# Splitting the attention burst around a matrix product in a fused attention and feed-forward kernel

## The chip, the cores and the metric

The kernel runs on one core of one Trainium2 chip. The metric is the device time of one execution in microseconds (us), the median over several executions; lower is better. One further execution was taken by the hardware profiler, and all rows shown come from it.

The names of the engines are those of the profile: PE is the matrix engine (its weight loads are listed apart, as PEld), DVE, ACT and POOL are the vector, scalar and general engines, SP is the queue from which most DMAs are issued. Each engine works through its own instructions strictly in the order of the program. They wait for each other by semaphores.

## The reference: what is computed

Sparse attention for 8 batches and 8 heads (576 positions, 64 values a head), followed by a feed-forward layer with a maximum over three products:

```python
scores = scale * np.matmul(q, k.transpose(0, 1, 3, 2))
mask_local = (rel >= 0) & (rel < stride)            # heads 0 to 3, stride 32
mask_strided = (rel >= 0) & (pos[None, :] % stride == pos[:, None] % stride)   # heads 4 to 7
attn = np.exp(scores - max) / (sum + 1e-09)
x = (attn @ v) laid out as 4608 tokens x 512
h = np.maximum(np.maximum(x @ w1, x @ w2), x @ w3)   # 768 wide
out = h @ w_out
```

## The kernel before

**Units.** Attention is cut into 32 units, numbered 0 to 31: a unit is two heads of one batch. In every batch the two strided pairs of heads come first, then the two local ones. One unit goes through these steps:

- `scores(n)` on PE: 32 or 36 small products into the PSUM tile `s_ps` (lines 340 and 318), each of them two passes, so the profile counts 64 or 72.
- `less_maximum(n)` on DVE (lines 361 to 368), `exponentials(n)` on ACT (line 384), `probabilities(n)` and `transposed(n)` on DVE (lines 394 to 404). The last one writes the probabilities to the SBUF tile `pt`. There is one `s_ps` from chunk two on, so the scores of a unit have to wait until the unit before has been transposed.
- `values(n)` on PE: probabilities times values into the PSUM tile `o_ps` (lines 441 and 470, 84 or 64 passes). There is one `o_ps` for all units.
- `leading(n)` on ACT: copies out of `o_ps` into the tokens' places (line 495). `rest(n)` does nothing for units from chunk two on.
- `paired_queries(n)`: for strided units, four ACT copies that lay out the queries (line 295); `scores(n)` reads them.
- `load_qk` and `load_v`: DMAs from SP for a unit two later, each of which waits until the unit whose buffer it takes has been used.

**The feed-forward part** runs in chunks of tokens. Chunks one and two (512 tokens each) are plain: 18 steps `ff_in` of 12 matrix instructions (line 522), each followed by `ff_max` that empties its PSUM bank, and 4 steps `ff_out` (line 552). Everything after that is done in four supers of 896 tokens. A super is 63 products of 6 matrix instructions of 448 columns (line 775, the weights of each come from HBM through `load_next`, eight ahead), then 7 output steps (line 865). Each product's result is copied out by ACT (`snap`, line 818), combined on POOL (line 830) and DVE (line 832). Two PSUM banks, `f_ps`, take turns for all of this.

**How the two are woven.** The order of the program is written out by hand. During chunk two and the supers, one unit of attention at a time is placed between products as a burst. In chunk two the table `first_bursts` gives the step i before which a unit's burst stands (units 8 to 15, two or three steps apart); a super has a burst before its products 8, 18, 28, 38, 48 and 58 (units 16 to 31 in three supers; `COUNTS` gives their number). The function `burst(n)` issues `values(n)`, `scores(n + 1)`, the loads, `leading(n)` and `less_maximum(n + 1)` in that order, and the softmax of unit n + 1 follows behind the next products.

During chunk two, ACT and POOL also build sums of weights for the supers: `build_sums` and `build_mix` on POOL (lines 585 and 593) at the steps of `sums_at`, three steps later `build_high` on ACT (line 603) and `build_low` on POOL (line 609).

## Time and profile before

| what | us |
|---|---|
| median of 3 runs | 690.41 |
| lowest and highest of them | 688.15, 691.15 |
| the profiled execution, whole | 694.4 |
| its span, first to last instruction | 692.7 |
| PE busy in it (94% of the span) | 653.0 |
| DVE, ACT, POOL busy | 376.7, 335.8, 299.6 |

The page of the profile gives, for each engine, the busy time; a chain of work followed back from the last instruction; and groups of instructions with the idle time before them. In a row of the timeline of an engine stand the start, the duration, the engine, the line of the kernel, the operation, its tiles and shape, how many equal instructions follow each other, and in brackets the idle time of the engine before the first of them with what ended it. "issue" there means that nothing in the profile explains the wait. In a row of the view of windows stand the stretch, its length, and for each engine its busy time and, in brackets, the number of its instructions; then the clock that PE was granted (1.00 is full) and two numbers on DMA.

### The profile page before, as it was taken

What the parts mean: (1) busy time and instruction counts of PE and PEld (TensorE: products, weight loads), DVE (VectorE), ACT (ScalarE), POOL (GpSimd) and SP (SyncE); (2) the same over time, 40 slices, a digit from 0 to 9 for tenths busy, and PEclk for the clock granted to TensorE, in tenths of its full rate; (3) what the DMA queues carried; (4) which work ended last, traced back from release to release, by engine and by line L of the source; (5) the groups of instructions that cost most, each with busy time, mean ns of one, the idle gap of its engine ahead of it and who ended that gap; (6) DMA issues with size and microseconds to landing.
All of it is one profiled execution on the core that took longest, in us unless ns stands there. A gap on an engine that the chain in (4) does not pass through costs nothing.

```text
span 692.7 us, 18051 instructions
## 1 busy us (share of the span) xinstructions
PE 653.0 (94%) x7408; PEld 560.6 (81%) x7408; DVE 376.7 (54%) x515; ACT 335.8 (48%) x702; POOL 299.6 (43%) x291
## 2 busy tenths in 40 slices
PE   3679999898999998999999999999999999999997
PEld 3458878686877888888898988889899988999986
DVE  5776965466766664567616556671653264124240
ACT  4757556333444544545555445464444454444441
POOL 8769898569970432322033432201433410444410
PEclk9679999899999999999999999999999999999999
DMA  9799883555778777764168777524867722777411
GB/s 289 201 281 348 283 265 117 173 164 171 241 239 261 248 265 220 248 222 164 62 198 279 241 243 232 171 76 142 251 203 199 214 91 91 214 216 219 142 46 62
DMA packets 89370, 138.36 MB, mean 200 GB/s; under 512 B 10152, under 2 KB 39592, under 8 KB 89288
## 3 DMA queue, kind: packets, MB, share of 16 engines
q1 hardware_dynamic: 85256, 129.86, 60.6%
q10 hardware_dynamic: 4032, 7.34, 2.8%
q8 instruction: 59, 0.97, 0.6%
q14 instruction: 23, 0.19, 0.1%
HBM read 111.21 MB, written 25.95 MB: 198 GB/s over the span
## 4 chain that ended last, share of the span: by engine, by line
PE 76%; DVE 7%; DMA 6%; issue 6%; SPq 2%; ACT 2%; POOL 1%; DVEq 0%; ACTq 0%; POOLq 0%
PE f_ps L775 40%; PE f_ps L865 15%; PE f_ps L522 10%; DMA w<-in_w 5%; PE f_ps L552 4%; PE o_ps L470 2%; PE o_ps L441 2%; PE s_ps L318 2%; PE s_ps L340 1%; DVE h_all L832 1%; POOL snap L830 1%; DVE xc L686 1%; DVE s_ps L397 1%; DVE pt L404 1%; SPq L280 1%
## 5 line engine op out<-in xcount | busy, mean ns | idle before, releaser
L775 PE MATMUL f_ps<-xc,w_stream 128*128 128x448 f32 x1512 | 316.5, 369 | 4.0 <-ACT snap L818 2.3
L775 PEld LDWEIGHTS f_ps<-xc,w_stream 128*128 128x128 f32 x1512 | 283.2, 189 | 31.6 <-ACT snap L818 4.7
L818 ACT COPY snap<-f_ps 128x448 f32<-128x448 f32 x240 | 127.7, 533 | 163.4 <-PE f_ps L775 161.6
L830 POOL TENSOR_TENSOR snap<-snap 128x448 f32<-128x448 f32 x72 | 89.6, 1252 | 161.1 <-ACT snap L818 102.9
L832 DVE TENSOR_TENSOR h_all<-h_all,snap 128x448 f32<-128x448 f32 x96 | 83.0, 907 | 115.9 <-POOL snap L830 115.8
L865 PE MATMUL f_ps<-wNone,h_parts 128*128 128x512 f32 x504 | 115.7, 390 | 0.9 <-ACT h_parts L855 0.9
L830 POOL TENSOR_TENSOR h_all<-snap 128x448 f32<-128x448 f32 x36 | 41.3, 1149 | 164.1 <-ACT snap L818 162.6
L865 PEld LDWEIGHTS f_ps<-wNone,h_parts 128*128 128x128 f32 x504 | 94.3, 188 | 21.5 <-ACT h_parts L855 1.7
L522 PE MATMUL f_ps<-xh,w 128*128 128x512 f32 x288 | 98.7, 416 | 3.4 <-ACT h_max L537 1.9
L522 PEld LDWEIGHTS f_ps<-xh,w 128*128 128x128 f32 x288 | 57.4, 199 | 17.6 <-ACT h_max L537 2.4
L522 PE MATMUL f_ps<-xl,w 128*128 128x512 f32 x144 | 59.0, 410 | 0.4 <-DVE xl L500 0.4
L856 DVE TENSOR_TENSOR h_parts<-h_all,h_parts 128x768 fp32r<-128x768 f32 (+2 forms) x40 | 27.2, 711 | 26.0 <-ACT h_parts L855 25.8
L686 DVE TENSOR_TENSOR xc<-x_block,xc 128x896 fp32r<-128x896 f32 x28 | 29.8, 1086 | 15.5 <-ACT xc L683 15.5
L871 ACT COPY work<-f_ps 128x512 f32<-128x512 f32 x28 | 16.4, 586 | 41.8 <-PE f_ps L865 41.8
L361 DVE TENSOR_TENSOR s_ps<-s_ps,mloc 128x640 f32<-128x640 f32 x14 | 11.6, 831 | 45.4 <-PE s_ps L340 45.3
L522 PEld LDWEIGHTS f_ps<-xl,w 128*128 128x128 f32 x144 | 28.9, 201 | 6.5 <-DVE xl L500 0.7
L404 DVE STREAM_TRANSPOSE pt<-s_ps 128x640 f32<-128x640 f32 (+2 forms) x32 | 32.5, 1016 | 1.1
L855 ACT CAST h_parts<-h_all 128x768 fp32r<-128x768 f32 (+2 forms) x40 | 24.5, 642 | 17.6 <-DVE h_all L832 11.0
L361 DVE TENSOR_TENSOR s_ps<-s_ps,mpair 128x576 f32<-128x576 f32 x14 | 10.7, 765 | 40.3 <-PE s_ps L318 40.3
L384 ACT ACTIVATE s_ps<-s_ps 128x640 f32<-128x640 f32 (+2 forms) x30 | 19.5, 652 | 26.7 <-DVE s_ps L368 26.7
L340 PE MATMUL s_ps<-qk_t 64*32 64x64 f32 (+1 forms) x1408 | 19.8, 227 | 12.7 <-DMA qk_t<-in_kT 8.5
L552 PE MATMUL f_ps<-wNone,hh 128*128 128x512 f32 x96 | 30.7, 400 | 0.0
(87 smaller groups left out, 709.5 us busy)
## 6 DMA issues: line engine op xcount, KB each, us to landing
w_stream<-scratch SPq DMA_DIRECT2D x252, 256.0 KB, 3.8
w<-in_w SPq DMA_DIRECT2D x18, 512.0 KB, 5.4
qk_t<-in_qT SPq DMA_DIRECT2D x28, 288.0 KB, 3.5
qk_t<-in_kT SPq DMA_DIRECT2D x28, 288.0 KB, 3.8
v_t<-in_v_str SPq DMA_DIRECT2D x56, 128.0 KB, 3.5
out<-work ACTq DMA_DIRECT2D x28, 256.0 KB, 2.0
scratch<-w SPq DMA_DIRECT2D x27, 256.0 KB, 3.6
v_t<-in_v_loc SPq DMA_DIRECT2D x48, 96.0 KB, 2.6
```

The source lines that it names most:

```text
L340: pin(nc.tensor.matmul(s_ps[32 * j : 32 * (j + 1), h, k1 : k1 + w], t[hs, q0 : q0 + 32], t[hs, k0 : k0 + w], start=not first, stop=not fir ...
L404: pin(nc.vector.transpose(pt[:, :, : nm * at], s_ps[:, :, : nm * at]))
L522: pin(nc.tensor.matmul(f_ps, w[:, kc, :], x[:, kc, :], start=(kc == 2 and n == 0), stop=(kc == 1 and n == 2)))
L552: pin(nc.tensor.matmul(f_ps, h[:, ts], w, start=(j == 0 and n == 0), stop=(j == NJ - 1 and n == 2)))
L686: pin(nc.vector.tensor_tensor(out=x[m][:, 1], in0=src, in1=x[m][:, 0].bitcast(F32), op=ALU.subtract))
L775: pin(nc.tensor.matmul(out_, w[:, wl, fs], x[:, xl, k, :], start=start and k == 0 and n == 0, stop=k == 1 and n == 2, skip_group_check=not ...
L818: pin(nc.scalar.copy(out=t, in_=src))
L830: pin(nc.gpsimd.tensor_tensor(out=h if i == 0 else u, in0=u, in1=t, op=ALU.add))
L832: pin(nc.vector.tensor_tensor(out=h, in0=h, in1=u, op=ALU.max))
L855: pin(nc.scalar.copy(out=to[:, 0, j0:j1], in_=src))
L856: pin(nc.vector.tensor_tensor(out=to[:, 1, j0:j1], in0=src, in1=to[:, 0, j0:j1].bitcast(F32), op=ALU.subtract))
L865: pin(nc.tensor.matmul(outs[t], h, w, start=(j == 0 and n == 0), stop=(j == NJ - 1 and n == 2)))
```

## The change

`burst` is taken apart. `ahead(n)` now issues the scores of unit n, its load of queries and keys and `less_maximum(n)`; `placed(n)` issues the values of unit n, the load of later values, and `leading(n)`. `ahead(n + 1)` stands where the burst of unit n stood. `placed(n)` stands one step (chunk two) or one product (supers) later. In chunk two, `paired_queries` is also moved ahead of `ff_max`. The work itself is the same, instruction for instruction, apart from two waiting instructions fewer on PE. Unit 15's values keep their place.

```diff
     def ahead(n):
-        if n < len(units):
-            scores(n)
-            list(load_qk(n + 2))
-
-    def burst(n, alone=False):
+
+        scores(n)
+        list(load_qk(n + 2))
+        less_maximum(n)
+
+    def placed(n):
 
         values(n)
-        coming = n + 1 if n + 1 < len(units) and not alone else None
-        if coming:
-            scores(coming)
         list(load_v(n + 2))
         leading(n)
         rest(n)
-        if coming:
-            list(load_qk(coming + 2))
-            less_maximum(coming)
-        return coming
...
     for i in range(3 * NJ + CH // P):
+        if i - 1 in first_bursts and first_bursts[i - 1] < 15:
+            placed(first_bursts[i - 1])
         if i in first_bursts:
-            coming, since = burst(first_bursts[i], first_bursts[i] == 15), i
+            if first_bursts[i] < 15:
+                coming, since = first_bursts[i] + 1, i
+                ahead(coming)
+            else:
+                placed(15)
         if i < 3 * NJ:
             ff_in(1, i // 3, i % 3)
         else:
...
         if coming and i == since + 1:
             probabilities(coming)
             transposed(coming)
+            if (coming + 1) % 4 in (0, 1):
+                paired_queries(coming + 1)
+            coming = None
         if i < 3 * NJ:
             ff_max(1, i // 3, i % 3)
         else:
             ff_store(1, i - 3 * NJ)
-        if coming and i == since + 1:
-            if (coming + 1) % 4 in (0, 1):
-                paired_queries(coming + 1)
-            coming = None
...
         def before(s, k):
 
+            n = 16 + sum(COUNTS[:s]) + k // 10
             if s == 0 and k == 1:
-                scores(16)
-                list(load_qk(18))
-                less_maximum(16)
+                ahead(16)
                 running[:] = [16, k]
             elif k % 10 == 8 and k // 10 < COUNTS[s]:
-                running[:] = [burst(16 + sum(COUNTS[:s]) + k // 10), k]
+                running[:] = []
+                if n + 1 < len(units):
+                    ahead(n + 1)
+                    running[:] = [n + 1, k]
+            elif k % 10 == 9 and k // 10 < COUNTS[s]:
+                placed(n)
 
         def after(s, k):
 
-            if running and running[0]:
+            if running:
                 n, since = running
```

How the rows move, at two places. The first is PE in the first super, around products 27 to 29, where the burst of unit 18 stood (L441 are its values, L340 the scores of unit 19, L775 or L774 the products). Before:

```order
L775 MATMUL f_ps_790<-xc_2972,w_stream 128x448 x6
L441 MATMUL o_ps<-pt,v_t 64x64 x14
L441 MATMUL o_ps<-pt,v_t 64x32 x8
L441 MATMUL o_ps<-pt,v_t 64x64 x14
L441 MATMUL o_ps<-pt,v_t 64x32 x6
L340 MATMUL s_ps<-qk_t 32x64 x36
L775 MATMUL f_ps_791<-xc_2966,w_stream 128x448 x6
L775 MATMUL f_ps_790<-xc_2967,w_stream 128x448 x6
```

The change, at the same place:

```order
L774 MATMUL f_ps_790<-xc_2972,w_stream 128x448 x6
L340 MATMUL s_ps<-qk_t 32x64 x36
L774 MATMUL f_ps_791<-xc_2966,w_stream 128x448 x6
L441 MATMUL o_ps<-pt,v_t 64x64 x14
L441 MATMUL o_ps<-pt,v_t 64x32 x8
L441 MATMUL o_ps<-pt,v_t 64x64 x14
L441 MATMUL o_ps<-pt,v_t 64x32 x6
L774 MATMUL f_ps_790<-xc_2967,w_stream 128x448 x6
```

The scores now stand alone ahead of a product, and the values alone behind it: one stretch of 78 small products (156 passes) has become one of 36 and one of 42.

The second place is ACT near the end of chunk two, steps 14 to 18 (L542 and L537 empty PSUM for `ff_max`, L603 is `build_high`, L384 the exponentials of units 14 and 15, L495 the copies `leading` of units 13 and 14). Before:

```order
L542 CAST hh<-h_max 128x512
L603 CAST sums_high<-work 128x512 x2
L495 COPY x_block_1927<-o_ps 128x192
L495 COPY x_block_2554<-o_ps 128x384
L384 ACTIVATE s_ps<-s_ps 128x2x320
L537 COPY h_max<-f_ps_790 128x512
L495 COPY x_block_1927<-o_ps 128x160
L495 COPY x_block_1927<-o_ps 128x32
L495 COPY x_block_2554<-o_ps 128x128
L495 COPY x_block_2554<-o_ps 128x160
L495 COPY x_block_2554<-o_ps 128x96
L384 ACTIVATE s_ps<-s_ps 128x2x320
```

The next two rows there are again L542 and L603.

The change, from the same row on:

```order
L542 CAST hh<-h_max 128x512
L603 CAST sums_high<-work 128x512 x2
L384 ACTIVATE s_ps<-s_ps 128x2x320
L537 COPY h_max<-f_ps_790 128x512
L495 COPY x_block_1988<-o_ps 128x192
L495 COPY x_block_2616<-o_ps 128x384
L384 ACTIVATE s_ps<-s_ps 128x2x320
L542 CAST hh<-h_max 128x512
L603 CAST sums_high<-work 128x512 x2
L495 COPY x_block_1988<-o_ps 128x160
L495 COPY x_block_1988<-o_ps 128x32
```

The copies of unit 14 (the last rows) now stand behind the second `build_high`, and the exponentials of unit 14 directly behind the first.

## The prediction

> **What bounds the kernel now.** I read the page first: who is busy, what the chain of work that ended last consists of, and the DMA queues.

> ```profile
> PE 653.0 (94%) x7408; PEld 560.6 (81%) x7408; DVE 376.7 (54%) x515; ACT 335.8 (48%) x702; POOL 299.6 (43%) x291
> ...
> q8 instruction: 59, 0.97, 0.6%
> ...
> PE 76%; DVE 7%; DMA 6%; issue 6%; SPq 2%; ACT 2%; POOL 1%; DVEq 0%; ACTq 0%; POOLq 0%
> ```

> PE sets the end; a gain must come out of PE's gaps or its instructions. So next the timeline of PE alone, from chunk two on, for the gaps. These eight stand in or right behind a burst:

> ```profile
> 131.78 0.87 PE L318 MATMUL s_ps<-qk_t,pt 64*64 64x36 f32 x25 [1.87 <-issue]
> 157.11 0.32 PE L340 MATMUL s_ps<-qk_t 64*32 64x64 f32 x8 [1.32 <-issue]
> 247.85 0.54 PE L340 MATMUL s_ps<-qk_t 64*32 64x64 f32 x34 [0.37 <-issue]
> 264.49 2.02 PE L775 MATMUL f_ps<-xc,w_stream 128*128 128x448 f32 x5 [1.76 <-issue]
> 371.72 0.71 PE L318 MATMUL s_ps<-qk_t,pt 64*64 64x36 f32 x34 [0.52 <-issue]
> 401.95 0.68 PE L340 MATMUL s_ps<-qk_t 64*32 64x64 f32 x44 [0.87 <-issue]
> 418.35 0.32 PE L340 MATMUL s_ps<-qk_t 64*32 64x64 f32 x9 [1.27 <-issue]
> 497.47 0.88 PE L775 MATMUL f_ps<-xc,w_stream 128*128 128x448 f32 x3 [0.72 <-ACT snap L818]
> ```

> They come to 8.70 us. Most break off in the middle of equal scores, where no semaphore is waited for. What they are is told by counting PE's instructions from gap to gap in the view of windows (PE and PEld, in brackets):

> ```profile
> 131.78:157.11 25.33, 24.00 (x381) 19.48 (x381) 13.24 (x20) 8.11 (x17) 19.48 (x19) 0.88 0.53 162
> 247.85:264.49 16.64, 14.88 (x251) 13.60 (x252) 10.06 (x14) 6.82 (x16) 5.73 (x5) 0.99 0.70 227
> 371.72:401.95 30.23, 29.36 (x374) 26.15 (x374) 16.13 (x24) 14.27 (x30) 10.01 (x8) 1.00 0.75 244
> 401.95:418.35 16.40, 15.13 (x252) 13.44 (x252) 9.47 (x12) 6.81 (x16) 7.07 (x6) 1.00 0.74 226
> 418.35:497.47 79.12, 77.81 (x751) 67.42 (x750) 46.83 (x60) 40.29 (x78) 15.92 (x14) 1.00 0.56 175
> ```

> The sums are 762, 503, 748, 504 and 1501: 6 to 35 short of 768, 512, 768, 512 and 1536, all multiples of 256, and the rest are PE's waiting instructions, which this view leaves out. The queue of instructions on the page fits: 59 packets for 2 x 7408 instructions are 251 each. So PE's program arrives in blocks of 256, and these gaps are waits for the next block (the last row's label, ACT, names a copy out of the other bank; its place fits the count). A burst of 42 + 36 small products is 312 instructions and takes about 2 us (1.07 and 0.93 for the two halves in rows further down); a product of 12 instructions takes 1.22. Only in a burst are 256 instructions used up faster than they come.

> Two of the gaps cost more than their length. The view of windows has the granted clock, the chain the stretches behind them and undisturbed ones of the same size:

> ```profile
> 131.15:137.97 6.82, 6.18 (x38) 4.95 (x38) 2.29 (x3) 1.68 (x3) 5.67 (x7) 0.50 0.52 137
> 264.27:267.68 3.41, 3.19 (x9) 2.84 (x9) 1.13 (x2) 0.54 (x1) 0.00 (x0) 0.50 0.72 179
> ...
> 132.66 10.90 PE f_ps L522 x36
> 167.81 8.39 PE f_ps L522 x36
> 264.49 13.90 PE f_ps L775 x60
> 280.52 12.48 PE f_ps L775 x60
> ```

> Half the clock behind the gaps of 1.87 and 1.76 us, none behind 1.32: 2.51 + 1.42 us, and the 25 scores in 0.87 us instead of 0.42: 4.4 us together.

> [...] If those dips had another cause, the sum below would lack their 4.4 us.

> **The change part by part.** Three waits in chunk two are for softmax, not for code:

> ```profile
> 164.27 1.17 PE L441 MATMUL o_ps<-pt,v_t 32*64 32x64 f32 x84 [1.14 <-issue]
> 166.40 1.41 PE L318 MATMUL s_ps<-qk_t,pt 64*64 64x36 f32 x64 [0.95 <-ACT pt L295]
> 195.13 1.13 PE L441 MATMUL o_ps<-pt,v_t 32*64 32x64 f32 x84 [0.90 <-issue]
> ...
> 163.32 0.85 DVE L404 STREAM_TRANSPOSE pt<-s_ps 128x640 f32<-128x640 f32 x1
> 164.78 0.62 ACT L542 CAST hh<-h_max 128x512 fp32r<-128x512 f32 x1 [3.95 <-DVE h_max L539]
> ```

> *Code waits.* The scores' and the values' instructions (128 to 168 each) now have a product between them. Two waiting instructions fewer leave the block borders where they were to within two, so those that cut into the scores now cut into the values, with a product ahead of them. The stretch before the border grows by 1.22 us and the 0.19 derived below, 1.41 (two matrix steps, more still, in chunk two). That swallows all gaps but the 1.76, which leaves 0.35; behind the one at 497.47 there was a product ahead of the border already, and I leave 0.30 of it. Gain 8.70 - 0.65 = 8.05. Ends: nothing (the next block is asked for as much later) and 8.70. I take a value near the upper end, because the border moves by a counted number of instructions.

> *Clock.* The longest gap left is 0.35, far under 1.32, behind which the clock held: gain 4.4, ends 0 and 4.4.

> *Waits for softmax.* The values at 164.27 started when the transpose had ended (164.17). Now that the scores stand ahead of the values, a unit's softmax begins 1.07 us earlier against PE, and its successor's scores, which need the same transpose, come where they stood: 1.14 falls to about 0. The queries at 166.40 waited behind `hh`, which waited 3.95 us for DVE; they are moved in front of it: 0.95 to 0. Gain 2.1, ends 0 and 2.1. The third, 0.90, would go likewise, but POOL takes its place:

> ```profile
> 154.81:199.70 44.89, 40.57 (x785) 33.26 (x777) 29.99 (x42) 16.97 (x43) 43.32 (x44) 1.00 0.65 200
> ...
> 184.56 3.18 POOL L593 TENSOR_TENSOR work<-work 128x256 f32<-128x256 f32 x4
> ...
> 187.88 1.14 ACT L603 CAST sums_high<-work 128x512 fp32r<-128x512 f32 x2
> 191.25 0.69 ACT L384 ACTIVATE s_ps<-s_ps 128x640 f32<-128x640 f32 x1 [1.64 <-DVE s_ps L368]
> ...
> 191.97 0.83 DVE L394 TENSOR_REDUCE s_ps<-s_ps 128x10 f32<-128x640 f32 x1 [0.81 <-ACT s_ps L384]
> 194.17 0.85 DVE L404 STREAM_TRANSPOSE pt<-s_ps 128x640 f32<-128x640 f32 x1
> ```

> POOL is busy 43.32 of 44.89 us there, and ACT's `build_high` started 0.14 us after its input was done (187.74). PE will be about 7.0 us earlier by then (1.87 + 0.45 + 2.51 + 1.32 + 2.1, less 1.2 for five splits), while POOL's chain, which follows PE's first steps of chunk two, moves by 1.87 + 0.45 + 2.51 less a split, 4.5. So `build_high` waits until about 183.2. Queued behind it on ACT are the exponentials of unit 14; then DVE must sum, scale and transpose, and PE's scores of unit 15 wait for that: 183.2 + 1.14 + 0.69 + 3.05 (191.97 to 195.02) = 188.1, where PE arrives at 194.23 - 7.0 + 0.19 = 187.4. A wait of 0.7 for one of 0.90: I take no gain, ends -2 and 0.9. Further on, the copies of unit 14 stand behind the next `build_high`, and the values of unit 15 need `o_ps` back; by the same count they are free when PE comes.

> *What splitting costs.* Values stand alone in one place of the trace, the last unit's. The view of windows, cut at products:

> ```profile
> 520.42:521.64 1.22, 1.22 (x7) 1.13 (x6) 1.22 (x3) 0.53 (x1) 0.00 (x0) 1.00 0.76 193
> 521.64:522.95 1.31, 1.31 (x7) 0.94 (x6) 0.27 (x1) 0.53 (x1) 0.00 (x0) 1.00 0.73 224
> 522.95:524.02 1.07, 1.07 (x85) 1.03 (x84) 0.00 (x0) 0.53 (x1) 0.00 (x0) 1.00 0.79 249
> 524.02:525.36 1.34, 1.34 (x12) 1.24 (x7) 0.00 (x0) 0.83 (x4) 0.00 (x0) 1.00 0.75 217
> 525.36:526.60 1.24, 1.24 (x8) 1.13 (x6) 0.00 (x0) 0.53 (x1) 0.38 (x1) 1.00 0.20 23
> ...
> 293.00 1.07 PE o_ps L470 x64
> 294.07 0.93 PE s_ps L318 x64
> ```

> The product ahead of small ones takes 0.09 more, the one behind 0.10. A burst pays that once, its two halves twice: 0.19 for each of 22 bursts (units 8 to 14 and 16 to 30), 4.2. Where strided values are followed by strided scores, the pair also shares something: 0.93 for scores that take 1.07 otherwise; 0.14 for six pairs, 0.8. Loss 5.0, ends 4.2 and 6.

> *DMA and ACT.* `load_qk` moves ahead of one `load_next` on SP, `load_v` behind it, at most some 2 us either way; weights are fetched eight products, 10 us, ahead and units two ahead. `leading` now runs during the product behind the values instead of during the scores, and that product's own copy comes only at its end. Nothing for both; if that cover went, each of 22 bursts could lose some tenths.

> Sum: 8.05 + 4.4 + 2.1 - 5.0 = 9.5 gained, 694.4 to 684.9 for the profiled execution. The runs' median is 4.0 below it. The gaps depend on when a DMA arrives, and the dips on the longest gaps, so part of that difference is likely gaps which ordinary runs have not: I put half the dips there and expect 7.4 off the median, 690.4 to **683.0**. Own range: 679 (all of the sum, and the third wait too) to 686.5 (a gain of 4).

> **The rivals.**
> 1. *POOL holds chunk two back.* If its chain moves by half of what I take, `build_high` waits 2.2 us longer, the wait at PE passes the length behind which the clock dipped (1.4), and some tenths are lost at unit 15. For it: the busy row. Against: POOL's chain starts behind an ACT copy that PE's first steps release. 683.0 + 4 = 687.
> 2. *The blocks stay late* (slower). Half a burst is still 128 to 168 instructions in about 1 us. If the next block is asked for no earlier ahead of the border in time than before, each border finds its wait again, one product later. It decides once a block comes over 1.4 us later than in the rows above. Gain 2.1, loss 5.0: 693.3. Against: the count of instructions fixes the border, and the earlier half runs ahead of it.
> 3. *Ordinary runs have few of these gaps.* If the 4.0 us are mostly clock dips and gaps, a third of the code waits remains to be won: 2.7 + 2.1 - 5.0, so 690.6. For it: the profiled execution is slower than all three runs.

> [...]

> **How the numbers follow.** My case 0.62, rival 1 0.13, rival 2 0.12, rival 3 0.13. About 0.5%, 3.5 us, is what a measurement here can tell from no change: faster means under 687.0, slower over 693.9. Faster: nearly all of my case and some of rival 1, 0.66; slower: nearly half of rival 2 and a tail of rival 3, 0.08; same 0.26. The range 679 to 690.5 takes in my case, rival 1 and half of rival 3, about 8 in 10.

> **What would show it.** Right: no gap over 0.5 us inside scores or values from chunk two on, clock 1.00 throughout, 22 products more than before at 1.31 and at 1.32 to 1.34, the gaps at step 9 gone, one of about half a us ahead of the scores of unit 15 with POOL's sums ahead of it. Wrong: "issue" gaps of over 1 us inside the values (rival 2), ACT idle for over 2 us ahead of `build_high` (rival 1), or a gain in the profile that the median does not have (rival 3).

## The result and the profile after

The changed kernel takes 684.65 us (median of 15 runs, 682.12 to 688.01), the kernel before beside it 691.15 (687.99 to 697.28). The ratio is 0.9898, 95% interval 0.9871 to 0.9925: 1.0% faster, where 683.0 against 690.4 had been forecast. The profiled execution has a span of 681.6 us against 692.7, with a mean granted clock of 0.987 against 0.975.

From the page of the changed kernel, busy time and the chain of work that ended last:

```profile
PE 649.3 (95%) x7408; PEld 554.2 (81%) x7408; DVE 371.2 (54%) x515; ACT 335.9 (49%) x702; POOL 299.8 (44%) x291
...
PE 71%; POOL 9%; DMA 6%; issue 6%; DVE 4%; SPq 3%; ACT 2%; POOLq 0%; DVEq 0%; ACTq 0%
```

PE has the same 7408 products. POOL, 1% of the chain before, now has 9% of it: in chunk two PE has come up to POOL.

Next the view of windows, cut at the same products in both kernels (chunk two, here from the last output step of chunk one on, then the first three supers with their outputs; the columns are length, then busy time and instructions of PE, PEld, DVE, ACT and POOL, the granted clock, the DMA share and GB/s; the last line sums all four). Before:

```profile
120.93:223.27 102.34, 93.99 (x1450) 75.88 (x1448) 62.82 (x87) 40.83 (x91) 68.19 (x68) 0.97 0.66 207
...
sum 443.76, PE 428.84 PEld 370.97 DVE 249.72 ACT 206.88 POOL 166.05; mean PE 107.21 PEld 92.74 DVE 62.43 ACT 51.72 POOL 41.51
```

After:

```profile
118.28:215.99 97.71, 92.43 (x1450) 73.22 (x1448) 63.05 (x87) 41.03 (x91) 68.28 (x68) 1.00 0.70 218
...
sum 435.27, PE 427.61 PEld 366.34 DVE 243.99 ACT 207.11 POOL 166.42; mean PE 106.90 PEld 91.59 DVE 61.00 ACT 51.78 POOL 41.60
```

So the part that the change touches got 443.76 - 435.27 = 8.5 us shorter. PE's idle time there fell from 14.9 to 7.7, its busy time by 1.2 (less half clock, more splitting). The other 2.65 us (120.93 to 118.28) lie ahead of chunk two, where nothing was changed; a wait that only the execution before had is one of them:

```profile
51.38 0.50 PE L522 MATMUL f_ps<-xh,w 128*128 128x512 f32 x1 [1.86 <-ACT h_max L537]
```

What is left of PE's waits from chunk two on, in the timeline of PE after (start, length, operation, and in brackets the idle time before it with what ended it); two more, of 0.40 and 0.59 us in output steps, were 0.30 and 0.59 before:

```profile
119.07 0.50 PE L552 MATMUL f_ps<-wNone,hh 128*128 128x512 f32 x1 [0.39 <-issue]
126.54 1.41 PE L318 MATMUL s_ps<-qk_t,pt 64*64 64x36 f32 x64 [1.90 <-ACT pt L295]
186.23 0.97 PE L340 MATMUL s_ps<-qk_t 64*32 64x64 f32 x72 [0.67 <-DVE pt L404]
196.30 1.53 PE L441 MATMUL o_ps<-pt,v_t 32*64 32x64 f32 x84 [0.65 <-ACT pt L295]
215.99 1.28 PE L774 MATMUL f_ps<-xc,w_stream 128*128 128x448 f32 x5 [1.67 <-ACT snap L821]
257.35 0.31 PE L441 MATMUL o_ps<-pt,v_t 32*64 32x32 f32 x5 [0.79 <-issue]
498.43 0.24 PE L340 MATMUL s_ps<-qk_t 64*32 64x64 f32 x1 [0.43 <-issue]
```

Three "issue" gaps of 1.6 us in all are left for eight of 8.7 us, one of them at a place where one stood before, and the clock is 1.00 from 50.8 us to the end of the work. But three waits in chunk two, 1.90, 0.67 and 0.65, are new or moved.

| term, us in the profiled pair | predicted | measured |
|---|---|---|
| waits for code, 8.70 before | 8.05 gained | 7.09 (1.61 left) |
| half clock behind two gaps | 4.4 gained | 4.4 |
| waits for softmax in chunk two | 2.1 gained | 0.55 (0.78, 1.14, 0.95, 0.90 became 1.90, 0.67, 0.65) |
| start of the first super, output steps | 0 | 0.38 lost (1.39 became 1.67, 0.30 became 0.40) |
| 22 splits | 5.0 lost | 3.17 lost (not measured by itself: what is left of the 8.5) |
| sum | 9.5 | 8.5 |
| medians | 7.4 | 6.5 |

### The profile page after: what moved, and what is told of

Same layout as the page of the kernel before. It is cut to its first block, busy times and chain, and to the rows that moved or that the text cites. A ratio compares the mean times of both kernels' runs of the same rounds, so it can differ in the third digit from the quotient of the medians.

```text
span 681.6 us, 18034 instructions
## 1 busy us (share of the span) xinstructions
PE 649.3 (95%) x7408; PEld 554.2 (81%) x7408; DVE 371.2 (54%) x515; ACT 335.9 (49%) x702; POOL 299.8 (44%) x291
## 4 chain that ended last, share of the span: by engine, by line
PE 71%; POOL 9%; DMA 6%; issue 6%; DVE 4%; SPq 3%; ACT 2%; POOLq 0%; DVEq 0%; ACTq 0%
PE f_ps L774 40%; PE f_ps L868 15%; PE f_ps L522 8%; DMA w<-in_w 4%; PE f_ps L552 3%; POOL work L593 2%; PE o_ps L441 2%; POOL work L609 1%; POOL work L585 1%; PE s_ps L318 1%; POOL snap L833 1%; PE o_ps L470 1%; DVE h_all L835 1%; PE s_ps L340 1%; DMA out<-work 1%
## 5 line engine op out<-in xcount | busy, mean ns | idle before, releaser
L774 PE MATMUL f_ps<-xc,w_stream 128*128 128x448 f32 x1512 | 317.7, 368 | 1.8 <-ACT snap L821 1.8
L774 PEld LDWEIGHTS f_ps<-xc,w_stream 128*128 128x128 f32 x1512 | 280.8, 188 | 28.0 <-ACT snap L821 3.9
L835 DVE TENSOR_TENSOR h_all<-h_all,snap 128x448 f32<-128x448 f32 x96 | 77.7, 847 | 127.3 <-POOL snap L833 127.0
L522 PE MATMUL f_ps<-xh,w 128*128 128x512 f32 x288 | 97.4, 407 | 1.8 <-ACT xh L495 1.8
L522 PEld LDWEIGHTS f_ps<-xh,w 128*128 128x128 f32 x288 | 55.7, 194 | 14.9 <-ACT xh L495 2.3
L522 PE MATMUL f_ps<-xl,w 128*128 128x512 f32 x144 | 57.7, 401 | 0.1
L404 DVE STREAM_TRANSPOSE pt<-s_ps 128x640 f32<-128x640 f32 (+2 forms) x32 | 32.5, 1016 | 1.1
L522 PEld LDWEIGHTS f_ps<-xl,w 128*128 128x128 f32 x144 | 27.9, 194 | 5.9 <-DVE xl L500 0.6
L384 ACT ACTIVATE s_ps<-s_ps 128x640 f32<-128x640 f32 (+2 forms) x30 | 19.5, 651 | 23.3 <-DVE s_ps L368 23.3
L340 PEld LDWEIGHTS s_ps<-qk_t 64*32 64x32 f32 x1408 | 16.3, 114 | 17.1 <-DMA qk_t<-in_qT 8.2
L340 PE MATMUL s_ps<-qk_t 64*32 64x64 f32 (+1 forms) x1408 | 19.5, 227 | 10.1 <-DMA qk_t<-in_kT 7.6
```

The lines of the kernel that those rows point to most:

```text
L340: pin(nc.tensor.matmul(s_ps[32 * j : 32 * (j + 1), h, k1 : k1 + w], t[hs, q0 : q0 + 32], t[hs, k0 : k0 + w], start=not first, stop=not fir ...
L404: pin(nc.vector.transpose(pt[:, :, : nm * at], s_ps[:, :, : nm * at]))
L522: pin(nc.tensor.matmul(f_ps, w[:, kc, :], x[:, kc, :], start=(kc == 2 and n == 0), stop=(kc == 1 and n == 2)))
L774: pin(nc.tensor.matmul(out_, w[:, wl, fs], x[:, xl, k, :], start=start and k == 0 and n == 0, stop=k == 1 and n == 2, skip_group_check=not ...
L835: pin(nc.vector.tensor_tensor(out=h, in0=h, in1=u, op=ALU.max))
```

## The experiments

**Each half alone.** `two_only` is the changed kernel with the supers' bursts as before, `supers_only` the reverse:

```
-            elif k % 10 == 8 and k // 10 < COUNTS[s]:
-                ... ahead(n + 1)
-            elif k % 10 == 9 and k // 10 < COUNTS[s]:
-                placed(n)
+                running[:] = [burst(16 + sum(COUNTS[:s]) + k // 10), k]
```

> The split only in chunk two; the supers place their bursts as before. Theory (the change's gain is the sum of what the two traces show part by part): chunk two keeps its 4.6 us of the profile (code waits 2.8, clock 3.0, less about 1.2 for seven splits), the six code waits in the supers (5.5 us in the trace of before) are back, some of them with a clock dip; so 2.5 to 4.5 us under before, 0.9935 to 0.9965. Rival (the bursts of the supers are where ordinary runs lose): 0 to 1 us, ratio above 0.9985. Rival (chunk two is all of it, the supers' split pays for itself only): 6 us, 0.991.

> The split only in the four supers; chunk two as before. Theory: code waits of 4.3 us and the clock's 1.4 go, 15 splits cost 0.2 each, chunk two keeps its waits and its clock dip: 2 to 4 us under before, 0.994 to 0.997. Rival (the split costs in the supers what it brings): 0 to 0.5 us, above 0.999. Rival (chunk two is nothing in ordinary runs): 6 us, 0.991.

Measured: 686.34 us for chunk two alone, ratio 0.9924 (0.9889 to 0.9958); 687.93 for the supers alone, 0.9962 (0.9935 to 0.9989), against 692.25 for the kernel before. Both give something, and 0.76 and 0.38% add up to about the whole. By the medians chunk two is the larger part, a little over what was expected; the two intervals overlap. The timeline of PE in `two_only` shows the gaps back where bursts stand together, and the new waits of chunk two without the supers' split:

```profile
126.62 2.21 PE L318 MATMUL s_ps<-qk_t,pt 64*64 64x36 f32 x64 [2.44 <-ACT pt L295]
...
199.59 1.69 PE L441 MATMUL o_ps<-pt,v_t 32*64 32x64 f32 x84 [1.00 <-DMA v_t<-in_v_loc]
...
262.28 13.90 PE L788 MATMUL f_ps<-xc,w_stream 128*128 128x448 f32 x59 [1.70 <-issue]
...
415.68 0.32 PE L340 MATMUL s_ps<-qk_t 64*32 64x64 f32 x8 [1.53 <-issue]
```

All four were followed by half the clock here (scores in 2.21 us instead of 1.1).

**Are the gaps block borders?** Small products that are overwritten at once were put into chunk one's output step, so that every later instruction has a higher number:

```
         f_ps = bank()
+        if (c, t) == (0, 2):
+            for r in range(64):
+                pin(nc.tensor.matmul(f_ps[...], x[:D, :64], x[:D, S : S + 36], start=True, stop=True))
```

> The kernel before, with 64 small products of 64x36 repeated into a bank that is overwritten next, in chunk one's output step: 128 instructions of PE more ahead of chunk two, 1.1 us of work. Theory (the program comes in blocks of 256 instructions, and PE waits where a block ends inside a burst): every gap with no wait of its own, from chunk two on, stands at a place whose count from the first instruction has the same rest by 256 as before, which is 128 instructions earlier in the program; none of the eight places of before keeps its gap except by that count; again some 6 to 12 gaps, 5 to 12 us in all. Rival (the gaps belong to what PE does at these products: banks, semaphores, a DMA): the gaps stand at the same products as before.

The page counts 7536 products instead of 7408: each of the 64 is two passes, so this is 256 instructions, one whole block, and it can tell nothing but that 1.1 us of other work ahead does not move the gaps. Six of the eight stand at the very products of before, four of them here (25, 8, 34 and 9 small ones left of a burst, as in the rows of the kernel before); the 0.52 and the 0.87 did not come:

```profile
133.85 0.56 PE L318 MATMUL s_ps<-qk_t,pt 64*64 64x36 f32 x25 [1.73 <-issue]
158.10 0.32 PE L340 MATMUL s_ps<-qk_t 64*32 64x64 f32 x8 [1.41 <-issue]
...
254.04 0.54 PE L340 MATMUL s_ps<-qk_t 64*32 64x64 f32 x34 [0.92 <-issue]
...
423.61 0.32 PE L340 MATMUL s_ps<-qk_t 64*32 64x64 f32 x9 [1.61 <-issue]
```

So the run was made with half as many, `range(32)`: 7472 products, 128 instructions more.

> The kernel before, with 32 instead of 64 repeated small products: each is two passes in the trace, so this adds 128 instructions of PE ahead of chunk two (the 64 added 256, a whole block, and left every border at its product). Theory: the borders stand 128 instructions earlier in the program, and a gap comes where a border lies at least some 186 instructions into a burst. So the gaps behind the bursts' starts number 17, 25, 26 and 29 are gone (units' values of that number), as are the 1.87 in chunk two's first burst and the 1.32 in its third; new ones stand at unit 22 (border at 288 of the burst: over 1 us), at unit 30 (269: about 1), 27 (238: about 0.5), 19 (257: 0.5 to 1), in chunk two's second burst (260: about 1), and small or none (0 to 0.6) at 16, 18, 21, 24 and chunk two's fifth (187 to 213). Rival (the gaps belong to the products): the same products as before keep them.

The timeline of PE now:

```profile
143.93 0.35 PE L340 MATMUL s_ps<-qk_t 64*32 64x64 f32 x7 [1.50 <-issue]
...
265.03 0.86 PE L340 MATMUL s_ps<-qk_t 64*32 64x64 f32 x63 [0.52 <-issue]
...
417.61 0.18 PE L441 MATMUL o_ps<-pt,v_t 32*64 32x32 f32 x1 [1.44 <-issue]
433.61 0.67 PE L318 MATMUL s_ps<-qk_t,pt 64*64 64x36 f32 x30 [0.53 <-issue]
```

The gap that had 9 of 72 scores left of its burst now has one value and all 72 scores left, 73 instead of 9: 64 products, or 128 instructions, earlier. The gaps in chunk two's first and third burst and behind units 17, 23 and 25 are gone, others have come. That settles what they are: a gap stands at a fixed place in blocks of 256 instructions. Counting every instruction of PE in the traces, the waiting ones too, makes it exact. In the thirteen profiles, from 100 us on, 56 waits of over 0.3 us leave a rest of 193 or 194 when their place is divided by 256. The only other waits labelled "issue" leave 241 (the scores of unit 9 in `relief` and the kernels built on it) or 2 (1.14 and 0.90 before, ahead of the values of units 11 and 14). The last two went with their products: in `borders128` they leave 130. So they are waits for softmax, and the rest tells the two kinds apart.

Which borders cost how much was forecast worse: units 26 and 29, listed as free, still had 1.44 and 0.98 (at 168 and 159 instructions into the burst), unit 22 had 0.37 instead of over 1, unit 19 none instead of 0.5 to 1, unit 21 had 1.25, chunk two's last burst 1.41. In the kernels that shift nothing, borders 287 to 315 instructions into a burst that stands together had 0 to 2.2 us, at 186 to 258 had 0 to 1.9, and earlier ones none, but for 0.40 and 0.42 at one 160 into a burst (unit 22 in `best` and `loads`).

**What half the clock goes by.** The kernel before with extra work in the output steps, where PE runs full products:

```
+                if t == 3 and super_now[0] == 0:
+                    for r in range(5):
+                        pin(nc.tensor.matmul(outs[t][:64], hall[:64, 0, :64], hall[:64, 1, :512], ...))
+                if t == 3 and super_now[0] == 2:
+                    for r in range(128):
+                        pin(nc.tensor.matmul(outs[t][:64, :36], hall[:64, 0, :64], hall[:64, 1, :36], ...))
+                for r in range({(1, 3): 4, (1, 5): 8, (2, 3): 3}.get((super_now[0], t), 0)):
+                    pin(nc.scalar.copy(out=outs[t], in_=hall[:, 0, :512]))
```

> The kernel before with extra work for nothing but the clock, in the output steps of the supers, where PE runs full products for 29 us: in super 0 five products of 64x64 by 512 columns (a quarter of the array, about 7 us, no idle time); in super 1 four copies that PE must wait for (about 2 us idle between full products) and, two outputs later, eight (about 4 us idle); in super 2 128 small products (about 2 us) and then three copies (about 1.3 us idle). Theory A (the clock is set by how much of the array was used in a stretch of 3.4 us, idle or not): half the clock in or behind the seven quarter-array us of super 0 and behind super 2's stretch or the 4 us idle, none behind the 2 us idle between full products. Theory B (only idle time counts, with a limit between 1.3 and 1.9 us): none in super 0, half behind both idle stretches of super 1, none in super 2.

The sizes came out otherwise: 4.4 us of quarter-array products, idle times of 5.95 and 6.86 us, and 24 us for the small products, which all write one place. Neither theory holds as put. The view of windows of this kernel, cut at the 3.41 us by which the clock's records change (columns as above, the clock third from the end):

```profile
325.67:329.08 3.41, 3.41 (x10) 1.12 (x9) 3.22 (x4) 2.83 (x5) 0.00 (x0) 1.00 0.34 127
...
455.38:458.78 3.40, 0.00 (x0) 0.00 (x0) 3.25 (x4) 3.34 (x6) 0.00 (x0) 1.00 0.19 73
458.79:462.20 3.41, 2.41 (x6) 1.93 (x7) 0.00 (x0) 0.91 (x2) 0.00 (x0) 0.50 0.00 0
591.91:595.32 3.41, 3.41 (x62) 3.41 (x60) 2.23 (x3) 0.91 (x2) 0.00 (x0) 1.00 0.00 0
595.32:598.73 3.41, 3.41 (x36) 3.41 (x34) 0.00 (x0) 0.00 (x0) 0.00 (x0) 0.50 0.00 0
...
158.42:161.83 3.41, 1.96 (x120) 1.79 (x124) 0.99 (x2) 2.39 (x7) 3.17 (x5) 1.00 0.73 198
451.96:455.37 3.41, 1.88 (x9) 1.22 (x7) 2.96 (x4) 2.39 (x4) 0.00 (x0) 1.00 0.22 81
```

A quarter of the array, fed 512 columns at a time, held the clock (first row, and it stayed 1.00 behind it). Products of 36 columns lost it although PE was busy for all of the 3.41 us (591.91). An empty stretch lost it too. So neither idle time alone nor the used part of the array decides. The number of columns streamed does not either. The stretch at 158.42 has 120 small products, 5776 columns by their shapes, and was followed by half the clock; the one at 451.96 has as little busy time and at most nine products of 512 columns, 4608, and the clock held. What decides is not settled here; the last section has a count that fits most stretches.

**What splitting costs by itself.** The kernel before, split only at eight bursts of the supers whose border lies early (unit 31's values, alone anyway, move by one product too):

```
+SPLIT = (16, 19, 21, 22, 24, 27, 28, 30)
+                    ahead(n + 1) if n in SPLIT else burst(n)
```

> The kernel before, with the split only at eight bursts of the supers where no block border lies late in the burst (units 16, 19, 21, 22, 24, 27, 28, 30). Theory (a split costs about 0.2 us and pays only where it takes a gap): these eight bursts take 0.1 to 0.2 us more each in the profile, 0.8 to 1.6 us in all, no gap goes; ratio 1.000 to 1.0035. Rival (the split helps by itself, by the order of the small products or the clock): 1 to 2.5 us under before, 0.9965 to 0.9985.

Time: 692.64, ratio 0.9999 (0.996 to 1.0038), too wide to decide between the two. The windows over ten products and one burst tell more, here for units 22 and 28, before:

```profile
353.55:368.14 14.59, 14.59 (x217) 12.95 (x216) 7.52 (x12) 7.88 (x19) 4.69 (x4) 1.00 0.73 237
...
477.63:491.99 14.36, 14.36 (x190) 13.15 (x188) 7.39 (x12) 6.58 (x13) 4.69 (x4) 1.00 0.67 186
```

and with the needless split:

```profile
351.72:366.47 14.75, 14.75 (x217) 12.87 (x216) 7.51 (x12) 7.89 (x19) 4.72 (x4) 1.00 0.80 258
...
476.62:491.30 14.68, 14.68 (x189) 13.16 (x188) 7.38 (x12) 6.58 (x13) 4.68 (x4) 1.00 0.79 219
```

0.16 and 0.32 more; the eight, cut alike, come to 1.2 to 1.4 us, about 0.17 each. In this profile a split is a loss wherever it takes no gap away.

**The three waits that stayed in chunk two.** At the first, ACT and DVE in the timeline after:

```profile
124.95 0.58 ACT L557 COPY work<-f_ps 128x512 f32<-128x512 f32 x1 [4.43 <-DMA out<-work]
125.44 1.33 ACT L295 COPY pt<-qk_t 128x288 f32<-128x288 f32 x4
```

The queries of unit 9 are queued on ACT behind a store of chunk one that waits 4.43 us for a DMA. Before the change the scores came behind the values, late enough. At the third wait the row names ACT's queries, which the values do not read; SP's queue tells more:

```profile
188.42 2.36 SPq L613 DMA_DIRECT2D scratch<-work  x2
...
191.90 1.84 SPq L269 DMA_DIRECT2D v_t<-in_v_loc  x3
193.79 0.59 SPq L271 DMA_DIRECT2D v_t<-in_v_loc  x1
194.43 0.59 SPq L273 DMA_DIRECT2D v_t<-in_v_loc  x1
```

The last of unit 15's values was issued at 194.43, behind two stores that took SP from 188.42 to 190.78 (the profile has the second wait for POOL), and PE waited until 196.30. `relief` copies unit 9's queries one store earlier and takes one subtraction off POOL:

```
-... O3 E8 L7 T1 Q3 N8          (then paired_queries(9))
+... O3 E8 L7 T1 U9 Q3 N8
-            pin(nc.gpsimd.tensor_tensor(out=hl, in0=a, in1=hh.bitcast(F32), op=ALU.subtract))
+            less = nc.vector if (c, j) == (1, 3) else nc.gpsimd
+            pin(less.tensor_tensor(out=hl, in0=a, in1=hh.bitcast(F32), op=ALU.subtract))
```

> The changed kernel, with the queries of unit 9 copied ahead of the last store of chunk one (on ACT they stood behind a copy that waited 4.4 us for a DMA), and one subtraction of chunk two (1.3 us) moved from POOL to DVE. Theory (the three waits that stayed in chunk two, 1.89, 0.67 and 0.62, are ACT's queue at the first and POOL's chain at the other two, the last by way of SP's queue, where the values' loads stand behind POOL's stores): the three fall to under 0.5 together, 2.5 to 3.5 us off the changed kernel, ratio to before 0.984 to 0.987. Rival (the last two are not POOL's): they stay, only 1.5 to 2 us are won, 0.987 to 0.9885.

681.52 us, ratio 0.9882 (0.9844 to 0.992). The ratio lies in the rival's range (0.987 to 0.9885), the gain on the changed kernel by the medians, 3.1 us, in the theory's, and the interval holds both: the time does not decide. In its timeline the three waits are smaller, none gone, and the third now names the load:

```profile
131.62 1.14 PE L318 MATMUL s_ps<-qk_t,pt 64*64 64x36 f32 x64 [0.70 <-issue]
...
190.79 0.97 PE L340 MATMUL s_ps<-qk_t 64*32 64x64 f32 x72 [0.47 <-DVE pt L404]
...
200.56 1.63 PE L441 MATMUL o_ps<-pt,v_t 32*64 32x64 f32 x84 [0.39 <-DMA v_t<-in_v_loc]
```

1.56 us in all for 3.22. The fall of the first, by 1.0 or more, is clear; the changed kernel profiled a second time (`after_again`) has 1.73, 0.82 and 0.30, so the third varies by as much with nothing changed. What is left of the first goes with DVE's transpose of unit 8 (it ends at 131.52, just ahead of the row). That the second goes with POOL is argued, not shown.

**Splitting where it pays.** On top of `relief`, in the supers only six bursts split:

```
+SPLIT = (17, 18, 23, 25, 26, 29, 31)
+                    ahead(n + 1) if n in SPLIT else burst(n)
```

> The kernel with the three waits relieved, and in the supers only those bursts split whose block border lies 186 or more instructions into the burst and showed a gap (units 17, 18, 23, 25, 26, 29); nine bursts stand together again as before. Theory (a split costs 0.2 us, a border early in a burst costs nothing): 1.5 to 2 us under the kernel it is built on, no new gap over 0.3 us. Rival (bursts that stand together bring gaps or half the clock back elsewhere): 0 to 3 us slower than that one.

678.75 us, ratio 0.9841 (0.9807 to 0.9875), 2.8 us under `relief` by the medians, with overlapping intervals. One gap of 0.73 came back that had not been expected, in unit 20's burst (border at 215).

Then one piece of the first super's conversion earlier:

```
-            for _ in range((2, 0, 1, 1)[i - 3 * NJ]):
+            for _ in range((2, 1, 1, 1)[i - 3 * NJ]):
```

> The kernel before this one, and one more piece of the first super's conversion taken one output step earlier, while ACT and DVE idle: the wait of 1.67 us at the second product of super one, for a copy that stands behind the conversion, goes. Theory: 1 to 1.7 us under the kernel it is built on. Rival (the conversion waits for data that is not there earlier): no difference.

The wait of 1.67 us at the start of the first super is gone from the profile; the time, 678.63 and 0.9831 (0.9795 to 0.9866), does not show it.

Last, the stores of build 7 two steps later on SP, behind unit 15's loads:

```
         for n, x in enumerate(a_of[q]): ...
+        if q != 7:
+            store_build(q)
...
             placed(first_bursts[i - 1])
+            if first_bursts[i - 1] == 13:
+                store_build(7)
```

> The fastest kernel so far, with the stores of one pair of sums (build 7) issued on SP two steps later, behind the loads of unit 15's values, which stood behind them. Theory (the last wait of chunk two is the load, landing 1.7 to 2.3 us after its issue): the wait ahead of unit 15's values, 0.36 to 1.01 in the runs, is gone; 0.3 to 1 us. Rival (it is ACT's copies of unit 14 behind POOL): it stays at 0.3 to 1.

SP and PE in its timeline:

```profile
187.73 0.59 SPq L276 DMA_DIRECT2D v_t<-in_v_loc  x1
```

```profile
190.98 1.14 PE L444 MATMUL o_ps<-pt,v_t 32*64 32x64 f32 x84
```

The loads are out 3.2 us ahead of the values and the wait is gone, so it was the load. 675.38 us, ratio 0.9754 (0.9707 to 0.9801): faster than both kernels, and by the medians more below the version it is built on than its 0.4 us of wait explains, though the runs of the two overlap (672.58 to 682.41, and 674.77 to 679.52). Neither profile has half the clock from 48 us on, so that is not it. Of the 5.6 us between the two profiles 3.35 lie ahead of chunk two, where the two kernels are the same; why, the runs do not tell.

The changed kernel once more beside it:

> The changed kernel once more, on the same chip as the two others. Theory: ratio to before 0.987 to 0.9925 again, 4.5 to 7 us slower than the fastest version.

684.66 us, ratio 0.9875 (0.984 to 0.9909), as in the first comparison, and 9.3 us slower than the fastest version instead of the 4.5 to 7 expected.

The lengths of the two parts in all profiles, cut at the same products as in the section above (what lies ahead varied from 115.9 to 124.8 us, though little or nothing was changed there, and is left out; the medians are of different sets of runs, in which the kernel before had 690.9 to 692.25):

| kernel | chunk two, us | three supers with outputs, us | median, us |
|---|---|---|---|
| before | 102.3 | 341.4 | 691.15 |
| changed | 97.7 | 337.6 | 684.65 |
| changed, again | 97.1 | 336.4 | 684.66 |
| two_only | 102.9 | 342.2 | 686.34 |
| supers_only | 103.0 | 336.5 | 687.93 |
| needless | 102.7 | 340.4 | 692.64 |
| relief | 95.6 | 337.2 | 681.52 |
| selective | 97.6 | 335.3 | 678.75 |
| best | 93.6 | 335.6 | 678.63 |
| loads | 92.6 | 334.3 | 675.38 |

The profile of `two_only`, 691.2, is far above its median: the four half clocks just shown. Where the supers are split throughout they take 336.4 to 337.6, where only six bursts are, 334.3 to 335.6: that fits nine of the fifteen splits there being paid for nothing, one profile each. In `selective` the third wait was 1.04 us, and half the clock behind it; `best`, which differs from it ahead of the first super only, had 0.42 there and the clock throughout.

## Why the prediction was right, and where not

The time and its sign were right, by the reasons given: the two terms named as the source, code and clock, brought 11.5 us of the profile's 8.5 net, and the halves and the shifted borders show that the gaps are what they were said to be.

- **Code waits.** The step "that swallows all gaps but the 1.76, which leaves 0.35" held for seven of the eight gaps. The 1.76 left 0.79 instead of 0.35, more than the 0.5 that was to show the prediction right, and two borders that had no gap over 0.3 before came to 0.39 and 0.43: what a border costs varies from run to run (0.79 and 0.55 at the same one in two profiles of the changed kernel). 7.1 instead of 8.05. Rival 2, that half a burst still outruns its block, is refuted by the same rows.
- **Clock.** 4.4 us, as put. The condition in the text, a gap longer than some 1.4 us, was not the right one: the 1.90 us at 126.54 brought no half clock here (the stretch in which it began had ten full products), the 1.00 us in `two_only` did (two full products in its stretch; 0.50 behind it). The clock's edges in these traces lie 3.41 us or multiples of it apart, and such a stretch need not be idle to lose it: in `clock` PE was busy for all 3.41 us from 591.91 on, and the next stretch had 0.50.
- **Softmax.** The wait at the scores of unit 15 was put at 0.7 and measured at 0.67, for the reason given (POOL, then `build_high`). ACT sat idle for 2.30 us ahead of that `build_high`, over the 2 us named as a sign of rival 1, but the wait at PE stayed at 0.67 and the clock held there:

```profile
181.36 1.14 ACT L603 CAST sums_high<-work 128x512 fp32r<-128x512 f32 x2 [2.30 <-POOL work L593]
```

  The step that failed is the gain of 2.1. The 1.14 and the 0.95 did go, but the sum stopped there: the same reordering asks for unit 9's scores ahead of unit 8's values, 1.07 us earlier, when ACT had not yet copied their queries (0.78 became 1.90). 0.55 instead of 2.1.
- **DMA.** "Nothing for both" was wrong by 0.65 in this profile (0.30 in `after_again`). `load_v` one step later was weighed against the weights' lead, not against the stores that stand ahead of it on SP; with those moved, in `loads`, the wait was gone. As far as the stores wait for POOL, it is rival 1's mechanism at a place that it did not name.
- **Splits.** 0.19 for a burst was right within its hundredths: 1.41 for the product between the halves, where 1.22 is undisturbed. In the view of windows of the kernel after, cut at products:

```profile
282.45:283.76 1.31, 1.31 (x7) 0.94 (x6) 0.00 (x0) 0.53 (x1) 1.29 (x2) 1.00 0.71 203
283.76:284.83 1.07, 1.07 (x66) 1.03 (x65) 0.00 (x0) 0.53 (x1) 0.94 (x2) 1.00 0.80 205
284.83:286.24 1.41, 1.41 (x12) 1.04 (x6) 1.24 (x2) 0.00 (x0) 0.84 (x1) 1.00 0.40 92
286.24:287.31 1.07, 1.07 (x65) 1.02 (x64) 1.03 (x2) 0.53 (x1) 0.00 (x0) 1.00 0.81 274
287.31:288.63 1.32, 1.32 (x13) 1.24 (x7) 0.01 (x1) 0.70 (x2) 0.00 (x0) 1.00 0.98 357
```

  The sum of 5.0 was still too high. Part of it is the 0.14 that a strided pair shares: before the change, the products behind three of the four such pairs in the supers took 1.24 each instead of 1.22 until the next burst, which took about as much back, and why they did is open. At the 0.17 that `needless` measured, 22 splits come to 3.7; what is left of the 8.5 is 3.2. The half us between them stays open.
- **From profile to median.** About half of the 4.4 us of half clock was taken to be missing in ordinary runs, 9.5 to 7.4; 8.5 in the profile became 6.5 in the medians, near enough. Which part of the gain it is that the ordinary runs lack was not measured. Rival 3 (690.6) is refuted.

The errors went both ways, 0.95 and 1.5 too much gain, 1.8 too much loss, 0.4 forgotten; that the sum came out so close is partly luck. (The lower end of the own range, all of the sum and the third wait, is 680 and not 679; it changes nothing.)

## What to carry to other kernels

Where a tight run of small instructions shows gaps with no wait of their own, count instructions from gap to gap before looking for a semaphore (here they lay multiples of 256 apart, to within one); a product of long instructions placed between the small ones hid most of them here (7.09 of 8.70 us), at a price per cut (0.17 to 0.2 us), so cut only where a border falls late in the run (here from 186 instructions on, though some at 159 to 168 waited 0.40 to 1.44 us too). When work is moved earlier, follow every queue that its inputs stand in: here ACT behind a store, and SP's loads behind other stores, cost 1.8 us, most of which a few lines in another place won back.

## What the hardware showed that was not expected

```profile
127.73:131.14 3.41, 2.18 (x103) 1.90 (x104) 0.00 (x0) 2.45 (x8) 1.28 (x1) 1.00 0.33 108
```

After, as much idle time but ten full products, and the clock held:

```profile
122.49:125.90 3.41, 2.15 (x10) 1.45 (x8) 2.39 (x4) 0.94 (x3) 0.29 (x1) 1.00 0.58 221
```

With the chunk-two split alone, more busy time than in either, 84 small and two full products, and the clock halved:

```profile
198.00:201.41 3.41, 2.41 (x88) 1.81 (x87) 0.42 (x1) 3.26 (x9) 1.94 (x2) 1.00 0.76 221
```

Counted over the traces from 100 us on, without the clock experiment, a fit lets a small product count for about a twenty-third of a full one. Then 22 of the 23 stretches that were followed by half the clock had under 6.5 full products' worth (about 15 fit in), while three others had as little and kept it. The numbers are fitted to these traces, an estimate and not a rule: a twenty-third is less than a small product's share of the columns (36 of 512 are a fourteenth), and in the clock experiment a stretch of two full and 46 small products kept the clock. By that estimate a split helps the clock as far as each stretch then holds full products; it did not always do, since `two_only` and `selective` lost the clock in chunk two, where the bursts were split, behind waits of 1.0 to 2.4 us.

The other is how far the wait at one border varies: the same border (the one at 257.35 above) waited 0.79, 0.55, 0.79, 0.53, 0.56 and 0.27 us in six profiles, two of the changed kernel and four of versions built on it. Why it varies stays open.
